# A state-space scan and a gated feed-forward on one core: one weight piece joined by halves, a clip moved to VectorE, state decays moved to ScalarE

## Chip, core and metric

The kernel runs on one core of a Trainium2 chip. The metric is the device time of one execution in microseconds, as the median of several runs; lower is better. The profile shows one further execution. Its own time is the span from the first to the last instruction plus what lies around it.

## What is computed

The first half is a chunked state-space scan over x, a, B and C (4 batches, 8 heads, 768 positions, head size 32, state size 16); the second is a feed-forward with a sigmoid gate on its 3072 x 256 result. Cut to what matters:

```python
log_a = np.log(np.clip(a, 1e-06, 1.0))
for c in range(nc):                                  # chunks of 32 positions
    cum = np.cumsum(la, axis=-1)
    L = np.exp(cum[:, :, :, None] - cum[:, :, None, :]) * causal
    M = np.einsum('bhin,bhjn->bhij', Cc, Bc) * L
    y_intra = np.einsum('bhij,bhjd->bhid', M, xc)
    y_inter = np.einsum('bhin,bhnd->bhid', Cc, state) * np.exp(cum)[:, :, :, None]
    y[:, :, sl] = y_intra + y_inter
    state = decay_full * state + np.sum(Bx, axis=2)  # Bx: B x x, decayed to the chunk's end
x = y.transpose(0, 2, 1, 3).reshape(B * S, H * D)    # 3072 x 256
h = x @ w_in                                         # 256 x 2048
g = h * (1.0 / (1.0 + np.exp(-1.702 * h)))
return (g @ w_out).astype(np.float32)                # 2048 x 256
```

The two weight matrices and their product are the bulk of the arithmetic. The weights arrive as 64-bit floats.

## The kernel before

The positions are taken in six blocks of 512 rows (`g` from 0 to 5): 128 positions of each of the four batches. Within a block the scan works in two sides of 64 positions (`i` 0 and 1) and in pairs of batches (`p`; `PG` = 2 pairs make a block). For each block there is a scan part and a feed-forward part, and the scan of block g+1 is laid between the feed-forward matmuls of block g. All engines keep the order in which the program was written: `in_order` at the end ties each instruction to the one before it on its engine.

**The weights.** VectorE has to make 32-bit floats out of the 64-bit words. The columns come in ten pieces (`PIECES`): four of two column tiles and two of four for `w_in` (column tiles f = 0 to 15), four of four for `w_out`. Pieces 0 to 3 hold f = 0 to 7, piece 4 holds f = 8 to 11, piece 5 holds f = 12 to 15. For one piece the steps are `fields` step 0 (L203, the exponent's bits), `fields` step 1 (L206, the mantissa's bits), `clamp` on ScalarE (two instructions, L224 and L226), `rounded` (L231) and `join` (L245 puts the sign in, L251 writes the finished weights). `narrow(i)` runs `rounded` on piece i, `fields` step 0 of the next piece, `join` of piece i, and `fields` step 1 of the next. For pieces 2 and 4 the join is cut into two halves of two column tiles, but the rounding ahead of them covers the whole piece. When a join is done, the next piece is fetched into the buffer that has come free (`NEXT`, on SP's queue).

**The first block.** Its feed-forward is a plain one. `hidden(0, f)` (L809) makes column tile f of the hidden layer, two accumulation steps of two matmul passes each (for the late f cut into two or four column parts), and ScalarE applies the gate (L813). It takes one of the four PSUM banks named `ff`, so tile f waits for the gate of tile f-4. After certain f the dictionary `in_hidden[0]` holds work to be issued: after f = 4 the second half of the first states, the loads of block 1's C and B by POOL's queue and `narrow(4)`; after f = 5 `store_a`; after f = 6 `pick_a(PG)` and `narrow(5)`; after f = 9 `fan_all(PG)` (matmuls L411 and scans L449), `narrow(6)` and SP's loads of block 1's x and spread a. After the sixteen tiles, `project_all(0)` (L907) goes over f again, with the work of `in_project[0]` in between.

**The clipped decay factors.** `az1` (128 x 128) and `az` (32 x 768, all of a) are read by two loads on SP and clipped by POOL in one loop, L376 and a memset of each half-chunk's first column, L378. `pick_a` reads `az1`. `store_a` writes `az` to a scratch in HBM, on SP's queue; `spread` later reads the scratch back on SP's queue, broadcast over partitions, and the scans `decay` (L403) run over it. `az1` serves the first pair of block 1, so that it need not wait for the scratch.

**The states.** `decayed(g, i)` multiplies the state before side i by the decay over that side (L671, into the only buffer of the tile `old`). `carry_first` adds it to side 1 of block 0's state (L994, through `plus`); `keep(g, i)` combines it with the block's own increment (L688, two instructions), and `keep_both` does both sides. `weigh(p)` multiplies the decay matrix of a pair by the scores that TensorE made into the PSUM area `cb` (L629). `finish` then forms y: `inter` (L730) from the states, `intra` (L746) from the weighted decay matrices. For block 1 and later y lies in the same PSUM area as the scores (`area`, one buffer), so `inter` of block 1 can't start before both `weigh` calls have read the scores.

**The start.** `finish` for block 0 runs early, with `dense` fillers on TensorE (L432: two passes over 256 columns that write into unused halves of the y banks). `spare` is one of them: it stands between the copy of the first side (L758) and `inter`.

Of the kernel before, what the change touches and what calls it, by code (L numbers as in the profile page):

```python
# [16 lines left out]
P = 128  # L17
# [18 lines left out]
def kernel(  # L36
# [31 lines left out]
    nc = tc.nc  # L68
# [159 lines left out]
    def rounded(i, half=None):  # L228

        cols = columns(i, half)  # L230
        nc.vector.scalar_tensor_tensor(out=mantissa[i][:, cols].bitcast(FP32), in0=bits[i][0][:, cols],  # L231
                                       scalar=2.0 ** -32, in1=mantissa[i][:, cols],
                                       op0=ALU.mult, op1=ALU.add)
# [4 lines left out]
    def join(i, parts=1, only=None):  # L238

        name, f, n = PIECES[i]  # L240
        n //= parts
        low, m, p2 = bits[i][1], mantissa[i], power[i]
        for k in range(parts) if only is None else only:
            cols, fs = slice(k * n * DM, (k + 1) * n * DM), slice(f + k * n, f + (k + 1) * n)
            nc.vector.scalar_tensor_tensor(out=p2[:, cols], in0=low[:, cols], scalar=0x80000000,  # L245
                                           in1=p2[:, cols], op0=ALU.bitwise_and, op1=ALU.bitwise_or)
            if name == "in":
                dst, h = w_in[:, fs].rearrange("p f k e -> p (f k e)").unsqueeze(1), 1
            else:
                dst, h = w_out[:, :, fs].rearrange("p c f e -> p c (f e)"), 2  # L250
            nc.vector.scalar_tensor_tensor(  # L251
                out=dst, in0=m[:, cols].bitcast(FP32).rearrange("p (h e) -> p h e", h=h),
                scalar=2.0 ** -20, in1=p2[:, cols].bitcast(FP32).rearrange("p (h e) -> p h e", h=h),
                op0=ALU.mult, op1=ALU.mult)
        if k == parts - 1:
            for n in NEXT.get(i, ()):
                fetch(n)

    def narrow(i):
        rounded(i)  # L260
        if i > 2 and i + 1 < len(PIECES):
            fields(i + 1, (0,))
        join(i, 2 if i in (2, 4) else 1)
        if i + 1 < len(PIECES):
            fields(i + 1, (1,) if i > 2 else range(2))

# [104 lines left out]

    fans, flat = {}, {}

    def clip(t):

        nc.gpsimd.tensor_scalar(out=t, in0=t, scalar1=1e-6, scalar2=1.0,  # L376
                                op0=ALU.max, op1=ALU.min)
        nc.gpsimd.memset(t.rearrange(by_chunk, s=2)[:, :, :, 0], 0.0)  # L378

    def pick_a(p):  # L380

# [285 lines left out]
    def decayed(g, i):  # L667

        t = ssd.tile([P, NB, Q * D], FP32, tag="old", name=f"old{g}_{i}", bufs=1)
        e = i * H + H - 1  # L670
        nc.vector.tensor_tensor(out=t, in0=state[g][:, 0] if i else state[g - 1][:, 1],  # L671
                                in1=since[g][:, :, e:e + 1].to_broadcast([P, NB, Q * D]),
                                op=ALU.mult)
        return t
# [21 lines left out]
    def finish(pairs, steps=range(2)):  # L696


        g, first = divmod(pairs[0], PG)
        early = pairs[0] < PG  # L700
        if 0 in steps:
            if early:
                banks = begun_y["banks"] = [bank(f"y0_{i}") for i in range(4)]
                y = [t[:, :2 * P].rearrange("p (k i) -> p k i", i=H) for t in banks]
                begun_y[0] = [[y[2 * t + i] for t in range(NK)] for i in range(2)], set()
            else:
                both = area(f"y{pairs[0]}")[:, :, :len(pairs) * 2 * H].rearrange(
                    "p (s t) (k i) -> p s t k i", s=2, i=H)
                begun_y[pairs[0]] = [[both[:, i, t] for t in range(NK)] for i in range(2)] + [both], set()
        y, begun = begun_y[pairs[0]]  # L710

        def begin(i, t, parts):
            new = not begun & {(i, t, q) for q in parts}
            begun.update((i, t, q) for q in parts)
            return new

        def inter(n, p, ts=range(2)):

            b = place(p)[1]
            for k in range(2):  # L720
                for i in range(2):
                    if g == 0 and i == 0:
                        continue
                    old = (state[g][:, 0] if i else state[g - 1][:, 1])[:, b + k]
                    for r in range(R):
                        t = r // 2
                        if t not in ts:
                            continue
                        rows, to = slice(32 * r, 32 * r + 32), Q * D * (r % 2)
                        nc.tensor.matmul(  # L730
                            out=y[i][t][to:to + Q * D, 2 * n + k], lhsT=old[rows],
                            rhs=st[p]["CsT"][rows, k, SIDES[i]],
                            start=begin(i, t, range(Q * (r % 2), Q * (r % 2) + Q)), stop=early,
                            tile_position=(32 * r, to), skip_group_check=True)

        def spare():
            dense(begun_y["banks"][1][:, 2 * P:], 4, False)

        def intra(n, p, ts=range(2)):
            L = Ls[p]  # L740
            for k, t in [(k, t) for t in ts for k in range(2)] if early else [
                    (k, t) for k in range(2) for t in ts]:
                for q in range(HB):
                    h = t * HB + q
                    for i, side in enumerate(SIDES):
                        nc.tensor.matmul(  # L746
                            out=y[i][t][D * q:D * q + D, 2 * n + k], lhsT=rx[p][side, k, h],
                            rhs=L[side, k, h // Q, h % Q],
                            start=begin(i, t, (q,)), stop=not early, tile_position=(H * i, D * q),
                            skip_group_check=True)  # L750

        cols = slice(2 * first * P, 2 * (first + len(pairs)) * P)

        if first == 0 and g not in yT:
            yT[g] = ffn.tile([P, NK, TG], FP32, tag="yT", name=f"yT{g}")
        if early:
            def copied(i, t):
                nc.scalar.activation(  # L758
                    yT[g][:, t, cols].rearrange("p (k s i) -> p s k i", s=2, i=H)[:, i], y[i][t],
                    AF.Copy)  # L760

            if 0 in steps:
                for t in range(NK):
                    dense(begun_y["banks"][0][:, 2 * P:])
                    intra(0, pairs[0], (t,))
                return
            for t in range(NK):
                intra(1, pairs[1], (t,))
                copied(0, t)
                if t == 0:  # L770
                    spare()
                for n, p in enumerate(pairs):
                    inter(n, p, (t,))
                copied(1, t)
        else:
            for step in steps:
                for n, p in enumerate(pairs):
                    (inter, intra)[step](n, p)
            if 1 not in steps:
                return  # L780
            for i in range(2):
                nc.scalar.activation(  # L782
                    yT[g][:, :, cols].rearrange("p t (k s i) -> p s t k i", s=2, i=H)[:, i], y[2][:, i],
                    AF.Copy)
        state.pop(g - 1, None)
        for p in pairs:
            st.pop(p)
            Ls.pop(p)
# [336 lines left out]
    rows = a.rearrange("b h s -> (b h) s")  # L1125
    nc.sync.dma_start(out=az1[:, 0], in_=rows[:, P:2 * P].unsqueeze(0).to_broadcast([R, NB * NH, P]))
    nc.sync.dma_start(out=az.rearrange("p c s -> p (c s)"), in_=rows)
    for t in az1, az:
        clip(t)
    fields(0, (1,), 0)  # L1130
    rounded(0, 0)
    finish(range(PG), (0,))
# [30 lines left out]
            nc.sync.dma_start(out=scratch[:, i].rearrange("c r i -> r c i"), in_=az[:, :, side])  # L1163

    at(in_hidden[0], 4, lambda: gain(range(PG), (1,)), lambda: keep_first(1))
    at(in_hidden[0], 5, store_a)
    at(in_hidden[0], 4, lambda: load_blocks(1, "C", [nc.gpsimd], held=True),
       lambda: load_blocks(1, "B", [nc.gpsimd]))
    at(in_hidden[0], 6, lambda: pick_a(PG))
    at(in_hidden[0], 9, lambda: fan_all(PG))  # L1170
    for i, k, c in ((2, 1, 1), (3, 2, 2), (4, 4, 4), (5, 6, 8), (6, 9, 12), (7, 12, 15)):
        at(in_hidden[0], k, lambda i=i: narrow(i))
        at(in_hidden[0], c, lambda i=i: clamp(i + 1))
    at(in_hidden[0], 9, lambda: load(PG, "x"), lambda: load(PG + 1, "x"), lambda: spread(PG + 1),
       lambda: spread_rows(1), lambda: spread_rows(2))
# [6 lines left out]
       lambda: ends_turned(PG + 1), lambda: mask_blocks(PG), lambda: mask_blocks(PG + 1),  # L1182
       lambda: clip_rows(1), lambda: decay_rows(1), lambda: since_start(PG, nc.gpsimd),
       lambda: since_start(PG + 1, nc.gpsimd), lambda: narrow(9))
    at(in_project[0], 9, lambda: score(pairs), lambda: gain(pairs), carry_first, lambda: keep_both(1),
       lambda: weigh(PG), lambda: weigh(PG + 1))
    at(in_project[0], 13, lambda: finish(pairs, (0,)))
    at(in_project[0], 15, lambda: finish(pairs, (1,)))
    at(in_project[0], 13, lambda: mix_in(1),
# [198 lines left out]
```

## Time and profile before

| | |
|---|---|
| runs shown | 350.62, 349.68, 349.15 us; median 349.68 |
| profiled execution | 349.98 us, of which the span is 348.3 us |
| TensorE (PE) | 343.3 us busy, 99% of the span; granted clock 1.000 |
| weight loads (PEld) | 281.9 us, 81%, beside the matmuls |
| VectorE (DVE) | 257.7 us, 74% |
| ScalarE (ACT) | 150.1 us, 43% |
| POOL | 46.0 us, 13% |
| HBM | 21.99 MB read, 3.24 MB written |

The share of PE is a modelled one: the matmuls are pipelined, and their ends are set by a model. A stretch in which PE is reported as busy can still hold a short stop, and a stop is best read from the starts of successive matmuls. The averages of the other engines hide that VectorE is nearly full from the start to some 90 us and half idle at the end.

### The profile page before, as it was taken

To read this page: it belongs to the slowest core of one execution; us is meant where nothing else is said; L and a number is where in the kernel's file an instruction comes from. 1 tells how busy PE (TensorE), PEld (TensorE's weight loads), DVE (VectorE), ACT (ScalarE), POOL (GpSimd) and SP (SyncE) were. 2 spreads that over 40 slices of the span, in tenths; PEclk is the share of its full clock that TensorE was granted. 3 is DMA by queue.
4 is the path that set the end of the run, shared out by engine and by line. 5 is a ranking of instruction groups with operands and counts; after the bars stand their busy time and mean duration, and the time that the engine had idled before them with its cause. 6 is when DMAs were issued, how large, how long until landed. Compare 5 with 4: busy or idle time off the path is not lost.

```text
span 348.3 us, 8552 instructions
## 1 busy us (share of the span) xinstructions
PE 343.3 (99%) x3514; PEld 281.9 (81%) x3514; DVE 257.7 (74%) x486; ACT 150.1 (43%) x335; POOL 46.0 (13%) x82
## 2 busy tenths in 40 slices
PE   9999999999999999999999999999999999999996
PEld 6658974555788888888888888888888888899996
DVE  7899999999799897839985648985554654455463
ACT  6579664005354314744342543432444322554320
POOL 8305910300396000000000000000000000000000
PEclk9999999999999999999999999999999999999999
DMA  4699985614639000554122345120000120000221
GB/s 102 197 321 279 284 167 123 98 48 79 100 77 145 2 0 13 88 115 94 27 37 61 47 98 102 23 31 9 2 4 0 19 32 12 0 2 0 33 31 60
DMA packets 82831, 25.79 MB, mean 74 GB/s; under 512 B 68856, under 2 KB 81144, under 8 KB 82792
## 3 DMA queue, kind: packets, MB, share of 16 engines
q1 hardware_dynamic: 79912, 23.19, 31.3%
q0 software_dynamic: 1888, 1.74, 2.4%
q8 instruction: 27, 0.44, 0.5%
q10 hardware_dynamic: 992, 0.33, 0.4%
q14 instruction: 12, 0.10, 0.1%
HBM read 21.99 MB, written 3.24 MB: 72 GB/s over the span
## 4 chain that ended last, share of the span: by engine, by line
PE 92%; DVE 4%; DMA 1%; issue 1%; ACT 0%; POOL 0%; SPq 0%; DVEq 0%
PE acc L967 28%; PE X L865 19%; PE Y L875 14%; PE o L907 8%; PE acc L974 7%; PE h L809 6%; PE y L746 2%; PE cb L618 2%; PE y L730 2%; DMA bits<-in_moe_w_in_dram 1%; PE A L649 1%; DVE w_in L251 1%; DVE p L245 1%; DVE p L203 1%; PE ab L520 1%
## 5 line engine op out<-in xcount | busy, mean ns | idle before, releaser
L870 ACT ACTIVATE ac<-X 128x256 f32<-128x256 f32 x76 | 29.2, 384 | 79.7 <-PE X L865 79.3
L967 PE MATMUL acc<-mg,mw 128*128 128x256 f32 x192 | 54.5, 379 | 0.0
L994 DVE TENSOR_TENSOR gT<-Y,ac 128x512 f32<-128x512 f32 x38 | 26.2, 690 | 36.9 <-PE Y L875 33.5
L842 ACT ACTIVATE gT<-gT 128x512 f32<-128x512 f32 (+1 forms) x76 | 39.4, 520 | 31.7 <-DVE gT L994 31.0
L865 PE MATMUL X<-my,mi 128*128 128x256 f32 x152 | 45.1, 379 | 0.0
L994 DVE TENSOR_TENSOR gT<-Y,b 128x256 f32<-128x256 f32 x38 | 15.9, 419 | 34.1 <-PE Y L875 34.1
L967 PEld LDWEIGHTS acc<-mg,mw 128*128 128x128 f32 x192 | 36.5, 190 | 5.0
L809 PE MATMUL h<-yT,w_in 128*128 128x128 f32 (+2 forms) x202 | 36.8, 340 | 0.6 <-DVE w_in L251 0.6
L967 PE MATMUL acc<-gT,w_out 128*128 128x256 f32 x128 | 35.5, 379 | 0.0
L809 PEld LDWEIGHTS h<-yT,w_in 128*128 128x128 f32 x202 | 27.6, 191 | 8.7 <-issue 5.9
L865 PEld LDWEIGHTS X<-my,mi 128*128 128x128 f32 x152 | 28.0, 190 | 3.8
L907 PE MATMUL o<-gT,w_out 128*128 128x512 f32 x64 | 28.6, 597 | 0.0
L833 DVE TENSOR_TENSOR mg<-gT 128x512 f32<-128x512 f32 x40 | 27.3, 682 | 0.0
L967 PEld LDWEIGHTS acc<-gT,w_out 128*128 128x128 f32 x128 | 24.2, 190 | 3.4 <-ACT yT L782 0.2
L870 ACT ACTIVATE b<-X 128x256 f32<-128x256 f32 x38 | 14.6, 385 | 20.6 <-PE X L865 20.2
L865 PE MATMUL X<-yT,w_in 128*128 128x256 f32 x76 | 23.2, 389 | 0.0
L875 PE MATMUL Y<-yT,w_in 128*128 128x256 f32 x76 | 22.7, 381 | 0.0
L875 PE MATMUL Y<-my,mi 128*128 128x256 f32 x76 | 22.6, 379 | 0.0
L865 PE MATMUL X<-my,w_in 128*128 128x256 f32 x76 | 22.6, 381 | 0.0
L875 PE MATMUL Y<-yT,mi 128*128 128x256 f32 x76 | 22.5, 379 | 0.0
L907 PEld LDWEIGHTS o<-gT,w_out 128*128 128x128 f32 x64 | 11.8, 190 | 13.2 <-issue 12.4
L1026 POOL DMA_DIRECT2D out_dram<-ob x32 | 17.4, 553 | 26.4 <-DVE ob L1021 26.1
(146 smaller groups left out, 582.5 us busy)
## 6 DMA issues: line engine op xcount, KB each, us to landing
a<-scratch SPq DMA_DIRECT2D x18, 256.0 KB
bits<-in_moe_w_out_dram SPq DMA_DIRECT2D x8, 512.0 KB
x<-in_x_dram SPq DMA_DIRECT2D x20, 128.0 KB
bits<-in_moe_w_in_dram SPq DMA_DIRECT2D x8, 256.0 KB
bits<-in_moe_w_in_dram SPq DMA_DIRECT2D x4, 512.0 KB
out_dram<-ob SPq DMA_DIRECT2D x128, 16.0 KB
af<-in_a_dram SPq DMA_DIRECT2D x20, 64.0 KB
zC<-in_C_dram SPq DMA_DIRECT2D x36, 32.0 KB
```

Of the source, the lines that this page charges most:

```text
L618: nc.tensor.matmul(out=s["cb"][side, r, k].rearrange("p (q i) -> p q i", q=Q), lhsT=BT[rows, k, side], rhs=CT[rows, k, :, side], start=Tru ...
L809: nc.tensor.matmul(out=h[:, cols], lhsT=w_in[:, f, k], rhs=yT[g][:, k, cols], start=(k == 0 and e == 0), stop=(k == NK - 1), skip_group_ch ...
L833: nc.vector.tensor_tensor(out=t[:, 0:2], in0=B[:, :, 1], in1=B[:, 0], op=ALU.subtract)
L842: nc.scalar.activation(o, i, AF.Silu, scale=GELU_SCALE)
L865: nc.tensor.matmul(out=s["X"], lhsT=lhsT, rhs=rhs, start=i == "1", stop=i == "4", skip_group_check=True)
L870: nc.scalar.activation(copy, s["X"], AF.Copy)
L875: nc.tensor.matmul(out=o, lhsT=lhsT, rhs=rhs, start=s.pop("new", False), stop=i != "5", skip_group_check=True)
L907: nc.tensor.matmul(out=o[c], lhsT=w_out[:, c, f], rhs=gT[g, f // 2][:, f % 2], start=(f == 0), stop=(f == NF - 1), skip_group_check=True)
L967: nc.tensor.matmul(out=acc[g][0][i], lhsT=w, rhs=h, start=(j == 0 and (i, 0) in begins), stop=(j == NF // 2 - 1), skip_group_check=True)
L974: nc.tensor.matmul(out=o[k] if type(o) is list else o[:, cols], lhsT=h[:, cols], rhs=w, start=(j == 0 and (i, k) in begins), stop=(j == NF ...
L994: nc.vector.tensor_tensor(out=o, in0=v, in1=w, op=ALU.add)
L1026: (nc.sync if g else nc.gpsimd).dma_start(out=rows[:, b, :, cols], in_=t[32 * r:32 * r + 32, b * P:(b + 1) * P].rearrange("p (u e) -> p u ...
```

## The change

`narrow(4)` is written out: the rounding of piece 4 is cut into halves as the join already was, so that the first half goes through `rounded`, (`fields` step 0 of piece 5), `join` before the second half is rounded. The clip of `az` moves from POOL to VectorE and from before the hidden layer to just after `narrow(5)`, and `store_a`, which reads it, moves behind it; `az1` stays on POOL. For blocks 0 and 1, `decayed` is four ScalarE copies with a per-partition scale, one for each batch, in place of one VectorE multiplication; this touches `carry_first` and the two sides of `keep(1, ...)`. The order behind them becomes `weigh(PG)`, `keep(1, 0)`, `weigh(PG + 1)`, `keep(1, 1)`. The filler `spare` is dropped, and a `dense` into the first y bank is issued instead inside `intra` of the second pair, between the rows of its first and second batch.

```diff
     def narrow(i):
+        if i == 4:
+            for k in range(2):
+                rounded(i, k)
+                if k == 0:
+                    fields(i + 1, (0,))
+                join(i, 2, (k,))
+            fields(i + 1, (1,))
+            return
         rounded(i)
...
-        join(i, 2 if i in (2, 4) else 1)
+        join(i, 2 if i == 2 else 1)
...
-    def clip(t):
+    def clip(t, engine=nc.gpsimd):
...
         e = i * H + H - 1
+        if g < 2:
+            for b in range(NB):
+                nc.scalar.activation(t[:, b], (state[g][:, 0] if i else state[g - 1][:, 1])[:, b],
+                                     AF.Copy, scale=since[g][:, b, e:e + 1])
+            return t
...
-        def spare():
-            dense(begun_y["banks"][1][:, 2 * P:], 4, False)
...
+                if early and n and not t and k:
+                    dense(begun_y["banks"][0][:, 2 * P:])
...
-                if t == 0:
-                    spare()
...
-    for t in az1, az:
-        clip(t)
+    clip(az1)
...
-    at(in_hidden[0], 5, store_a)
...
+        if i == 5:
+            at(in_hidden[0], k, lambda: clip(az, nc.vector), store_a)
...
-    at(in_project[0], 9, lambda: score(pairs), lambda: gain(pairs), carry_first, lambda: keep_both(1),
-       lambda: weigh(PG), lambda: weigh(PG + 1))
+    at(in_project[0], 9, lambda: score(pairs), lambda: gain(pairs), carry_first, lambda: weigh(PG),
+       lambda: keep(1, 0), lambda: weigh(PG + 1), lambda: keep(1, 1))
```

More of the change, by code (lines that the diff above doesn't have):

```diff
@@ L372 @@
     fans, flat = {}, {}
-    def clip(t):
-        nc.gpsimd.tensor_scalar(out=t, in0=t, scalar1=1e-6, scalar2=1.0,
+    def clip(t, engine=nc.gpsimd):
+        engine.tensor_scalar(out=t, in0=t, scalar1=1e-6, scalar2=1.0,
                                 op0=ALU.max, op1=ALU.min)
-        nc.gpsimd.memset(t.rearrange(by_chunk, s=2)[:, :, :, 0], 0.0)
+        engine.memset(t.rearrange(by_chunk, s=2)[:, :, :, 0], 0.0)
     def pick_a(p):
```

## The prediction

> **What bounds the kernel now.** I read the busy shares first, then who waited for whom on PE, then the two places in the timeline where PE stopped.
>
> ```profile
> PE 343.3 (99%) x3514; PEld 281.9 (81%) x3514; DVE 257.7 (74%) x486; ACT 150.1 (43%) x335; POOL 46.0 (13%) x82
> ...
> DVE  7899999999799897839985648985554654455463
> ```
>
> PE is the bound nearly everywhere, and the change takes no matmul away. It can gain only where PE stops, and VectorE, full for its first 90 us, is the likely cause there. The waits of PE over the whole span are few:
>
> ```profile
> PE busy L439 <- PEq L1372: 0.8, 1, 0.8
> PE h L809 <- DVE w_in L251: 0.6, 1, 0.6
> ```
>
> The second line is the one that the change aims at. In the timeline from 28 to 34 us (start, length, engine, line):
>
> ```profile
> 28.61 1.22 DVE L231 SCALAR_TENSOR_TENSOR m<-bits,m 128x1024 f32<-128x1024 uint32 x1
> ...
> 29.75 0.78 DVE L203 TENSOR_SCALAR p<-bits 128x1024 uint32<-128x1024 uint32 x1
> ...
> 30.45 0.68 DVE L245 SCALAR_TENSOR_TENSOR p<-bits,p 128x512 uint32<-128x512 uint32 x1
> ...
> 30.91 2.84 POOL L376 TENSOR_SCALAR az<-az 32x768 f32<-32x768 f32 x1
> 31.16 1.20 DVE L251 SCALAR_TENSOR_TENSOR w_in<-m,p 128x512 f32<-128x512 f32 x1
> ...
> 32.51 1.69 PE L809 MATMUL h<-yT,w_in 128*128 128x128 f32 x13 [0.56 <-DVE w_in L251]
> ```
>
> Tile f = 8 starts when L251 has written the first half of piece 4 (31.16 + 1.20 = 32.36). PE's last matmuls before it started at 31.33, 31.44, 31.55 and 31.67, so the next was due at 31.78; it came 0.73 us late, and its successor took another 0.07 to fall back into step. **The stop costs 0.80 us.** Two things make it: 1024 columns are rounded where 512 were needed, and L251 took 1.20 instead of the 0.69 that its twin at 33.00 took; it started 0.25 us after POOL's long clip.
>
> The second stop is too short for the list of waits. The timeline before 73 us:
>
> ```profile
> 65.59 7.13 PE L907 MATMUL o<-gT,w_out 128*128 128x512 f32 x16
> ...
> 70.32 2.34 DVE L629 TENSOR_TENSOR L<-L,cb 128x1024 f32<-128x1024 f32 x2
> ...
> 72.81 1.35 PE L730 MATMUL y<-CsT,S 32*64 32x64 f32 x64
> ```
>
> Sixteen matmuls 0.43 apart from 65.59, with 0.1 for the switch at each end, make L730 due at 72.66. It came at 72.81: its PSUM area is the one that both `weigh` read, and these ended at 70.32 + 2.34 = 72.66. **This stop costs 0.15 us now**, and it would swallow anything that PE gains earlier unless VectorE comes earlier too.
>
> **Piece 4 by halves, and the clip off POOL: -0.80.** Times below are from start to start, since VectorE's instructions overlap a little. Rounding 512 columns takes 0.60 (25.35 to 25.95) against 1.14 for 1024 (28.61 to 29.75); L203 0.61 alone (25.95 to 26.56), 0.70 beside POOL's clip of `az1`; L245 0.72 and L251 0.61 (26.56, 27.28, 27.89). So from 28.61: rounding to 29.21, `fields` of piece 5 to 29.91 (taken at 0.70, since `az1` is still clipped by POOL), L245 to 30.63, L251 ends at 30.63 + 0.69 = 31.32. PE wants f = 8 at 31.78, less about 0.1 for the semaphore and the weight load: 0.35 us to spare. (VectorE's wait for the words of piece 5 ended at 29.06 in the trace, so they are there by 29.21, with 0.15 in hand; later words would eat into the 0.35.) Either half of the edit alone would leave little of the stop: the split alone ends L251 at 31.3 to 31.85, the clip alone at 31.85.
>
> What is late next? f = 9 needs the bank of f = 5, whose gate ScalarE ends at 33.39; f = 9 is then due at 31.78 + 1.82 = 33.60. That holds, narrowly, since ScalarE's own chain (clamp from 30.57 to 32.9) isn't moved. f = 10 needs the second half: L231, L245, L251 end near 32.65, PE comes there at 35.4. f = 12 needs piece 5: VectorE is 0.54 ahead by the rounding of piece 5 (33.80 against 34.34), so its join ends at 38.0; PE comes at 39.7 instead of 40.5.
>
> The clip of 32x768 on VectorE lies behind `narrow(5)`: between L489 (512 columns, 0.42) and L203 (1024, 0.69), say 0.57, and 0.07 for the memset (L493), 0.65 with their gaps. Queued behind it are the scans L449, `narrow(6)` and all of VectorE's list to 72 us. It spends the 0.54 just won: VectorE stands 0.1 later than before from 39 us on. `narrow(6)` ended at 45.62 for an f that PE takes at 47.68, 46.9 now: covered by over 1 us.
>
> On SP's queue `store_a` (0.82 us of issue at 34.38) moves behind the fetch at 37.33, to about 39.2, and x, the spread `a` and the rows `af` stand behind it:
>
> ```profile
> 38.32 7.33 SPq L146 DMA_DIRECT2D x<-in_x_dram  x4
> 45.75 2.02 SPq L282 DMA_DIRECT2D a<-scratch  x2
> 47.81 5.19 SPq L292 DMA_DIRECT2D af<-in_a_dram  x8
> ```
>
> They go 1 to 2 us later. The first readers on VectorE are the scan of `a` at 57.98 and L489 at 60.70, 10 us behind their issue; cost nothing. On POOL's queue the sixteen loads of C and B, which started at 34.62 behind the clip, start near 31.
>
> **The decays on ScalarE: they keep the 0.80 and add 0.15.** Off VectorE go three L671 (67.17, 68.08, 69.27; 0.45 to 0.54 from start to start): 1.4. Each becomes four copies of 128x64; no row has that shape. Bounds: 0.20 (128x1, L314) and 0.29 from start to start (128x128, L388), so 0.8 to 1.2 a decay, taken at 1.1, near the wider row, since a copy's fixed part weighs most. ScalarE has nothing from 58.6 to 79.2, so the first one is long done. From 67.28 on VectorE: `plus` to 67.74, `weigh` (1.13) to 68.87, L688 (68.62 to 69.27, 0.65) to 69.52, `weigh` to 70.65, ending about 70.75 instead of 72.66. The new waits are of L688: its decay starts when `plus` has ended (67.7) and takes to 68.8, so the first `weigh` hides it; the second is hidden by the second `weigh` to within 0.2. Behind a waiting L688 stand the `weigh` and so L730. PE wants the area at 72.66 - 0.80 = 71.86, less 0.1. Margin: 0.8 to 1.0. Both stops are then gone. Without this part 70.32 + 2.34 + 0.1 would hold PE to its old time, and the 0.80 would be lost.
>
> **The filler: 0.** PE's two passes at 14.50 to 15.13 (0.63) leave their place ahead of `inter` and come where PE waits for the second `weigh` of the pair: the rows before end near 13.61, the rows behind start at 13.90. They would then start near 14.35, 0.45 later, and `inter` 0.15 to 0.2 earlier. PE reaches `hidden` that much earlier, but f = 1 follows L251 at 17.89 (0.42), and that follows a DMA:
>
> ```profile
> 17.22 0.29 DVE L203 TENSOR_SCALAR p<-bits 128x256 uint32<-128x256 uint32 x1 [0.52 <-DMA bits<-in_moe_w_in_dram]
> ```
>
> f = 1 starts at 18.56 on time, when weights ready at 18.31 allow 18.45 at best; and f = 3 follows its own join (21.98) at 22.13. Bounds: 0.1 won, 0.2 lost if the rows come later than that; I take 0.
>
> **Sum:** -0.80 - 0.15 + 0 = -0.95. The profiled execution goes from 349.98 (span 348.3) to 349.03 (span 347.35). It lies 0.30 above the median of the runs, 349.68, so the forecast is 348.7. A measurement can tell about 0.5% (1.75 us) from no change: the gain, 0.27%, is under that.
>
> **Rivals.** *The wait moves to the score area* (349.6): if L688 waits for ScalarE, `weigh` ends later than 71.75 and L730 takes back what f = 8 gave. To lose all, a decay must take about 2 us, 0.5 a copy; no row of ScalarE up to 128x128 shows over 0.40. 0.12.
>
> *POOL's remaining clip blocks VectorE* (349.9, slower). The clip of `az1` starts at 29.24 and lasts 1.44, and `fields` of piece 5 now starts just there. If VectorE had to stand still for all of it, L203 would start at 30.7, L251 would end at 32.76, f = 8 would come at 32.87, 0.36 later than now; with the 0.15 won at 72, +0.2. It decides from 0.35 us of blocking on. Against it: L203 beside that clip took only 0.09 more than alone, and within the long clip the L245 at 32.28 and the L251 at 33.00 took 0.68 and 0.69; the most seen is the 0.51 of one L251. 0.10. The Trainium skill, SBUF — State Buffer, section Who interferes with whom, says that the two engines share a port pair and that the later one "fully blocks" until the earlier is done. By that rule this rival would be the forecast; but also the L251 at 31.16 should have stood until 33.75, and it ended at 32.36, so the trace agrees only in that there is interference.
>
> *The start gains too* (348.1): the filler's whole 0.63 comes off the path, if the first weights come earlier by chance of the DMA. 0.06.
>
> *The weights' DMA is pushed back* (350.6 and more): POOL's sixteen loads, 0.5 MB, now come 3.6 us earlier into a stretch where the DMA share is 0.92 to 1.04 and 290 to 305 GB/s move. The join of piece 5 stands behind `fields` of piece 6 on VectorE (due 34.9); if that piece lands after 36.6, f = 12 is late by as much, and beyond 37.6 the gain is gone. All sixteen loads ahead of it would cost 0.5 MB / 290 GB/s = 1.8 us, and L203 at 35.48 didn't wait. 0.08, half of it within 0.5%.
>
> **The numbers.** Forecast 0.64. The range 348.0 to 350.0 holds the forecast, the first three rivals and the partial losses between; it leaves out the last one and a gain over 1.7. Over 0.5% faster (below 347.9) is the far half of the start's rival (0.03) and a little for what the trace can't show: 0.04. Over 0.5% slower is the far half of the last rival (0.04) and as little: 0.05. Between: 0.91.
>
> **What would show it.** Right: no wait of PE on L251 near 32 us, f = 8 at 31.8; L251 of f = 8 at 0.69; VectorE's last `weigh` before 71.2 and L730 at 71.9; everything behind 0.95 earlier. Wrong: f = 8 still waits; L688 idles on ScalarE by more than 0.5; `hidden` starts after 16.8; a granted clock below 1.00 near 14 to 20 us.

## The result, and the profile after

| | before | after |
|---|---|---|
| time, median (us) | 349.71 (349.06 to 351.27, 17 runs) | 348.40 (347.87 to 349.6, 17 runs) |
| profiled execution, time / span (us) | 349.98 / 348.3 | 347.87 / 346.1 |

The ratio is 0.9963, with an interval of 0.9949 to 0.9977: 1.3 us less (0.8 to 1.8). That is under the 0.5% that the prediction took as the least to be told from no change, but the interval leaves no change out. The forecast was 348.7. Ratios here and below compare executions in the chip's usual state; the one of `early_piece1` that was profiled (2000 us) was not in it, so its trace is not read.

The first line of the page and the whole list of PE's waits in the kernel after:

```profile
PE 341.6 (99%) x3514; PEld 281.4 (81%) x3514; DVE 256.3 (74%) x486; ACT 152.5 (44%) x347; POOL 42.1 (12%) x80
...
PE busy L447 <- PEq L1382: 0.9, 1, 0.9
PE ab L528 <- DVE cum L377: 0.4, 1, 0.4
```

As many matmuls as before. The wait on L251 is gone from the list; a small one on L377, in a later stage, is new here, but a second trace of the same kernel doesn't have it. The timeline near f = 8:

```profile
27.63 0.69 DVE L231 SCALAR_TENSOR_TENSOR m<-bits,m 128x512 f32<-128x512 uint32 x1
28.04 1.12 POOL L384 TENSOR_SCALAR az<-az 128x128 f32<-128x128 f32 x1 [14.90 <-DMA az<-in_a_dram]
28.24 0.78 DVE L203 TENSOR_SCALAR p<-bits 128x1024 uint32<-128x1024 uint32 x1
28.95 0.68 DVE L245 SCALAR_TENSOR_TENSOR p<-bits,p 128x512 uint32<-128x512 uint32 x1
29.66 0.69 DVE L251 SCALAR_TENSOR_TENSOR w_in<-m,p 128x512 f32<-128x512 f32 x1
...
27.32 7.22 PE L819 MATMUL h<-yT,w_in 128*128 128x256 f32 x52
```

One half is rounded, the field of piece 5 is cut beside POOL's clip of `az1`, and L251 takes 0.69 and ends at 30.35. PE's hidden matmuls (last line) run through from 27.32 to 34.54 without a gap, f = 8 among them. The clip that VectorE has taken over, and SP's queue:

```profile
37.66 0.56 DVE L384 TENSOR_SCALAR az<-az 32x768 f32<-32x768 f32 x1
38.27 0.67 DVE L457 TENSOR_TENSOR_SCAN L<-ab,idents 128x256 f32<-128x256 f32 x1
...
38.38 0.82 SPq L1172 DMA_DIRECT2D scratch<-az  x2
39.24 5.33 SPq L146 DMA_DIRECT2D x<-in_x_dram  x4
44.68 1.49 SPq L290 DMA_DIRECT2D a<-scratch  x2
```

The clip holds VectorE's list for 0.61 us. The issue of `store_a` moved 4 us, but the spread `a`, which reads what it stored, is issued no later than before (44.68 against 45.75; counted from A, the mark explained below, 0.1 earlier), where the prediction had 1 to 2 us later. The score area of block 1, which PE takes over at `inter`:

```profile
63.82 7.13 PE L917 MATMUL o<-gT,w_out 128*128 128x512 f32 x16
...
66.68 1.21 DVE L637 TENSOR_TENSOR L<-L,cb 128x1024 f32<-128x1024 f32 x1
66.79 1.06 ACT L681 ACTIVATE old<-S,since 128x64 f32<-128x64 f32 x4 [8.01 <-DVE S L1004]
67.89 0.61 DVE L701 SCALAR_TENSOR_TENSOR S<-A,part,old 128x128 f32<-128x128 f32 x2
68.41 1.21 DVE L637 TENSOR_TENSOR L<-L,cb 128x1024 f32<-128x1024 f32 x1
68.59 1.06 ACT L681 ACTIVATE old<-S,since 128x64 f32<-128x64 f32 x4 [0.74 <-DVE S L701]
...
70.88 1.16 PE L743 MATMUL y<-CsT,S 32*64 32x64 f32 x64
```

Each decay takes ScalarE 1.06 us beside a `weigh` of 1.21, and no L701 waits. The second `weigh` ends at 69.62. Before, PE came 0.15 us after the `weigh` that held it (72.66 to 72.81), so it could have ended at 70.73 and not held PE: 1.11 us in hand.

**Where the time went.** The start differs from one execution to the next, so whole spans are poor evidence. I take one mark behind it: A, the first of the state matmuls that follow f = 4 (line L649 before, L657 after). Over all traces A lies between 24.9 and 26.8 us. The table counts from there: A to the first `inter` matmul of block 1, from that to the first matmul behind those 64, and all the rest (us, from the matmuls' records):

| kernel | A at | A to `inter` | the 64 | the rest |
|---|---|---|---|---|
| before | 25.88 | 46.92 | 1.28 | 274.19 |
| after | 24.91 | 45.97 | 1.09 | 274.16 |
| after, second trace | 25.33 | 45.97 | 1.09 | 274.17 |

The two traces of the changed kernel agree to 0.01, and the rest is what it was to within 0.03. Of the kernel before there is one trace. A to `inter` lost 0.95, and the 64 matmuls, which follow a stop before and none after, lost 0.19: **1.14 us in all**, against 1.3 (0.8 to 1.8) by the medians. Of the 2.1 us between the two profiled executions, the other 1.0 lies ahead of A.

### The profile page after: what moved, and what is told of

The parts are those of the page before. It is cut to its first block, busy times and chain, and to the rows that moved or that the text cites. A ratio compares the mean times of both kernels' runs of the same rounds, so it can differ in the third digit from the quotient of the medians.

```text
span 346.1 us, 8565 instructions
## 1 busy us (share of the span) xinstructions
PE 341.6 (99%) x3514; PEld 281.4 (81%) x3514; DVE 256.3 (74%) x486; ACT 152.5 (44%) x347; POOL 42.1 (12%) x80
## 4 chain that ended last, share of the span: by engine, by line
PE 97%; ACT 1%; ACTq 1%; DVE 0%; issue 0%
PE acc L977 28%; PE X L875 19%; PE Y L885 14%; PE h L819 10%; PE o L917 8%; PE acc L984 7%; PE y L758 3%; PE cb L626 2%; PE y L743 2%; PE A L657 1%; PE ab L528 1%; ACTq L130 1%; PE y L440 0%; ACT L322 0%; PE b L584 0%; ACT cum L373 0%
## 5 line engine op out<-in xcount | busy, mean ns | idle before, releaser
L411 DVE TENSOR_TENSOR_SCAN L<-a,idents 128x1024 f32<-128x1024 f32 x9 | 20.5, 2274 | 0.0
```

What stands on the lines that cost most here:

```text
L411: nc.vector.tensor_tensor_scan(out=L, data0=ra[p].rearrange("p k e -> p (k e)"), data1=idents.rearrange("p h i -> p (h i)"), initial=0.0, ...
```

## The experiments

My theory was that two stops hold PE, at f = 8 and at `inter`, and that the first is worth nothing while the second stands, because VectorE's `weigh` gives it back. The rivals were that the gain is the filler's, at the start, and that POOL's remaining clip takes some of it. I added each part to the kernel before, took each away from the kernel after, and then parted order and engine of the decays. All ratios are against the kernel before, run beside each group, so its median differs a little from group to group. Two sets are small: `order_only` has 7 runs and `no_filler` 5, the others 11 or more.

**Piece 4 by halves alone** (`split_only`): the kernel before with the new branch in `narrow`.

```diff
     def narrow(i):
+        if i == 4:
+            for k in range(2):
+                rounded(i, k)
+                if k == 0:
+                    fields(i + 1, (0,))
+                join(i, 2, (k,))
+            fields(i + 1, (1,))
+            return
```

> The kernel before, with only piece 4 rounded and joined by halves. Theory 1 (the gain of the change is two stops of PE, 0.80 us before tile f = 8 and 0.34 us at inter of block 1, and the filler gives nothing): the first half of piece 4 is joined 0.5 to 1.1 us earlier, so the stop before f = 8 falls from 0.80 to 0.1 or less; VectorE is 0.5 us ahead from there on (no clip is added to it), so the stop at inter doesn't swallow the gain but grows from 0.15 to about 0.35 us; in all 0.4 to 0.6 us faster than before. Theory 2 (half or more of the gain comes from the start, where the filler was moved): 0.3 us or less. If POOL's long clip slows whichever join instruction it meets by 0.5 us, L245 or L251 of the first half still takes 1.2 us.

Measured: 350.24 against 350.04, ratio 1.0004 (0.9985 to 1.0023). A miss. PE's wait at f = 8 is gone, but a longer one stands at `inter`; from its waits and its timeline:

```profile
PE y L738 <- DVE L L637: 1.7, 1, 1.7
...
31.50 3.20 POOL L384 TENSOR_SCALAR az<-az 32x768 f32<-32x768 f32 x1
32.00 1.31 DVE L245 SCALAR_TENSOR_TENSOR p<-bits,p 128x512 uint32<-128x512 uint32 x1
33.34 0.69 DVE L251 SCALAR_TENSOR_TENSOR w_in<-m,p 128x512 f32<-128x512 f32 x1
33.95 1.30 DVE L206 TENSOR_SCALAR m<-bits 128x1024 uint32<-128x1024 uint32 x1
```

POOL's long clip now met two other instructions: L245 took 1.31 instead of 0.69 and L206 1.30 instead of 0.69, while the L251 between them kept its 0.69. That is 1.2 us of VectorE's time, and it had also waited longer for words (0.77 us at 26.17; the stop of PE at f = 6 that followed cost 0.75, so PE came to f = 8 late by that much). The trace doesn't part these two; either way the delay was carried on for 40 us to the `weigh`.

**The clip alone** (`clip_only`): `clip(az)` and `store_a` as in the change, the rest as before.

> The kernel before, with only the clip of az on VectorE behind the join of piece 5 and the scratch store behind it. Theory 1: L251 of the first half of piece 4 takes 0.69 instead of 1.20 us, f = 8 comes 0.5 us earlier with a stop of 0.2 to 0.3 left; but VectorE pays 0.65 us for the clip, stands 0.1 us later than before at the scores, and PE waits there 0.6 to 0.8 us; in all no change, -0.1 to +0.2 us. Theory 2: no change either. If the loads behind the store on SP's queue come too late, VectorE idles before the scan at 58 us, and it is slower by that idle time.

Measured: 349.71 against 350.04, ratio 0.9992 (0.998 to 1.0003), as expected. L251 took 0.69 and the stop at f = 8 shrank from 0.80 to 0.32 (A to the fan-out matmuls, L411, took 9.88 against 9.56 without a stop). PE then stopped further on:

```profile
72.66 1.29 PE L730 MATMUL y<-CsT,S 32*64 32x64 f32 x64 [0.84 <-DVE L L629]
```

**The filler alone** (`filler_only`): only `spare` goes and `dense` comes into `intra`.

> The kernel before, with only the filler moved from ahead of inter into the second rows. Theory 1: hidden starts 0.1 to 0.5 us earlier, measured from the first score matmul, but f = 1 to f = 3 then wait for their weights, and the stop before f = 8 takes up whatever is left; no change, -0.1 to +0.1 us. Theory 2: 0.4 to 0.7 us faster.

Measured: 350.02 against 350.04, ratio 0.9994 (0.9981 to 1.0007), as expected. From the first score matmul to the first hidden matmul PE took 7.10 us instead of 7.58. Here that ended in a wait for the next words, which landed late:

```profile
18.14 0.29 DVE L203 TENSOR_SCALAR p<-bits 128x256 uint32<-128x256 uint32 x1 [1.49 <-DMA bits<-in_moe_w_in_dram]
```

**Without the new decays and order** (`no_decay`): the kernel after with `keep_both(1)` ahead of both `weigh` and the decays on VectorE.

> The changed kernel, with the decays of the states back on VectorE and the old order behind them (both sides of the state, then both weigh). Theory 1: f = 8 without a stop, 0.80 us won; VectorE ends the second weigh at its old time or 0.1 us later, so PE stops about 0.95 us before inter of block 1 and all but 0.1 us of the gain is given back; in all -0.2 to +0.1 us against the kernel before. Theory 2: 0.6 us or more remain, since the start was won before that.

Measured: 350.12 against 350.04, ratio 0.9998 (0.9987 to 1.0008), as expected. There is no stop at f = 8 (A to the fan-out matmuls takes 9.56); all of it comes back here:

```profile
72.31 1.16 PE L738 MATMUL y<-CsT,S 32*64 32x64 f32 x64 [1.04 <-DVE L L637]
```

So without the third part nothing is kept of the gain, but this part has two halves, the engine and the order.

**The order alone** (`order_only`): the kernel after without the branch that sends the decays to ScalarE. **The new decays and order alone** (`decay_only`): both halves put into the kernel before. **ScalarE in the old order** (`act_old_order`): the kernel after with this line back:

```diff
-       lambda: keep(1, 0), lambda: weigh(PG + 1), lambda: keep(1, 1))
+       ..., lambda: keep_both(1), lambda: weigh(PG), lambda: weigh(PG + 1))
```

> The changed kernel with the three decays back on VectorE, but in the new order behind them (weigh, side 0, weigh, side 1). Theory 1, sharpened by the runs so far (before the change PE is held at inter of block 1 by VectorE's unbroken chain, which runs from the landing of piece 1 to the second weigh; what shortens that chain counts until PE's own work is the longer): the new order takes one of the two state sides from ahead of the second weigh, two decays of about 0.48 us come back ahead of it; VectorE frees the scores about 0.2 us before PE wants them, so this kernel is as fast as the changed one, 1.0 to 1.3 us faster than before. Rival (moving the decays off VectorE is what matters): PE stops 0.5 us or more at inter, and no more than 0.7 us is won.

> The kernel before with only the decays on ScalarE and the new order. Theory 1: VectorE's chain is 2.2 us shorter, so inter of block 1 has no stop and its matmuls start at full pace; the stop before f = 8 stays at about 0.8 us; in all 0.3 to 0.6 us faster. Rival (VectorE's chain is all that counts, and the stop before f = 8 is nothing by itself): 1.0 us or more.

> The changed kernel with the decays on ScalarE, but the old order behind them (both sides of the state, then both weigh). Theory 1 (the new order, not the engine, frees the scores in time): nothing covers the 1.1 us that four copies take on ScalarE, so VectorE waits for them twice, about 2 us in all; the second weigh ends 1.5 us after PE wants the scores, PE stops there by that, and this kernel is 0.3 to 0.8 us slower than the one before. Rival (taking the decays off VectorE is what matters): 0.7 us or more faster than before.

Measured, `order_only`: 348.39 against 349.62, ratio 0.9967 (0.9955 to 0.998), as fast as the whole change, as expected. Its timeline:

```profile
70.10 0.61 DVE L696 SCALAR_TENSOR_TENSOR S<-A,part,old 128x128 f32<-128x128 f32 x2
70.63 1.21 DVE L637 TENSOR_TENSOR L<-L,cb 128x1024 f32<-128x1024 f32 x1
...
71.76 0.42 DVE L679 TENSOR_TENSOR old<-S,since 128x256 f32<-128x256 f32 x1
...
72.23 1.16 PE L738 MATMUL y<-CsT,S 32*64 32x64 f32 x64
```

The second decay (L679 at 71.76) stands behind the `weigh` instead of ahead of it. The `weigh` ends at 71.84, 0.24 us before it would hold PE; PE doesn't wait.

Measured, `decay_only`: 349.36 against 349.62, ratio 0.9994 (0.9982 to 1.0007); 0.3 less, where 0.3 to 0.6 was expected; the medians can't tell so little. The trace can. Behind the start this is PE's only wait:

```profile
PE h L814 <- DVE w_in L251: 0.6, 1, 0.6
```

There is no stop at `inter`, the one at f = 8 is as before, and from A to the end it takes 0.37 less.

Measured, `act_old_order`: 351.57 against 350.13, ratio 1.0038 (1.002 to 1.0056), 1.3 us slower than before. That is more than the 0.3 to 0.8 expected. From A to the end its trace is 0.68 longer; what it lost ahead of A (26.84, with 1.64 of waiting for words) can't be told from the scatter of the start. The timeline shows where the 0.68 comes from:

```profile
69.81 0.61 DVE L701 SCALAR_TENSOR_TENSOR S<-A,part,old 128x128 f32<-128x128 f32 x2 [1.13 <-ACT old L681]
71.61 0.61 DVE L701 SCALAR_TENSOR_TENSOR S<-A,part,old 128x128 f32<-128x128 f32 x2 [1.19 <-ACT old L681]
72.13 2.34 DVE L637 TENSOR_TENSOR L<-L,cb 128x1024 f32<-128x1024 f32 x2
```

With nothing between a decay and its reader, VectorE stands still for each, 2.3 us, and both `weigh` queue behind that. The decays on ScalarE are an advantage only in an order that hides them, and there they aren't needed.

**The filler in its old place, and none at all** (`no_filler_move`, `no_filler`): the kernel after with `spare` back, and without `dense` in `intra`.

> The changed kernel with the filler back in its old place ahead of inter. Theory 1: hidden starts 0.2 to 0.5 us later, counted from the first score matmul; up to f = 3 the weights hold PE as long, so the time is that of the changed kernel within 0.2 us, 1.0 to 1.3 us faster than before. Rival (with no later stop left to swallow it, an early hidden counts in full): 0.4 to 0.6 us slower than the changed kernel, 0.7 us faster than before.

> The changed kernel without the moved filler at all (that one dense is left out; it computes nothing that is used). Theory 1: hidden starts 0.3 to 0.5 us earlier still, and f = 1 to f = 3 wait for their weights; the time is that of the changed kernel within 0.2 us. Rival of the run before: 0.4 us faster than the changed kernel. If the filler keeps the clock up, the granted clock falls below 1.00 in the first 25 us and it is over 1 us slower.

Measured: 348.56 and 348.48, both against 349.62; ratios 0.9975 (0.9962 to 0.9988) and 0.9966 (0.9954 to 0.9978). Both intervals hold the change's own ratio. PE came to `hidden` 0.73 later than in the changed kernel and 0.12 earlier, counted from the first score matmul; neither lies where it was expected, and the time didn't follow. The granted clock of the run without the filler is 1.00. The filler isn't where the gain is.

**Weights asked for earlier** (`early_fetch`, `early_piece1`): the kernel after with the second half of piece 0 and piece 1 released ahead of the first `weigh`, and with only piece 1 released earlier, right behind piece 0. These try to win what the start loses to late words.

```diff
+    fetch(0, held=nc.vector, halves=(1,))
+    fetch(1, held=nc.vector)
...
-    fetch(0, held=nc.vector, halves=(1,))
...
-    fetch(1, held=nc.vector)
```

> The changed kernel with the loads of the second half of piece 0 and of piece 1 released ahead of the first weigh instead of behind it. Theory 1: with both later stops gone, what is left to vary is the start, and there VectorE waits for the words of piece 1 (0 to 1.5 us in the traces so far); the words come about 1.3 us earlier, the wait goes, tile f = 4 ends at 24.9 to 25.1 us in the trace, and the median is 0.3 to 0.7 us under the changed kernel's. Against it: the loads of x share the DMA engines then, and the first intra may wait for them; then no gain or a loss up to 0.5 us.

> The changed kernel with the load of piece 1 released right behind that of piece 0's second half, ahead of the two products of the end rows. Theory 1: piece 1 lands about 0.6 us earlier; half of the gain of the run before, 0.1 to 0.4 us under the changed kernel, without touching the loads of x.

Measured: 348.81 and 348.92 against 350.13; ratios 0.9967 (0.9951 to 0.9984) and 0.9968 (0.9955 to 0.9981). Both miss: they are no better than the change itself, whose ratio beside them (`after_again`) was 0.9964 (0.9949 to 0.9979). In `early_fetch` the wait for piece 1 is gone, but VectorE waited 0.40 us for words at 25.82 instead, which cost PE 0.3 between A and `inter`.

> The changed kernel once more, on the same chip as the three others, to compare them with it. Theory 1: from the state matmuls after f = 4 to the end the trace takes 321.2 us, as in the first trace of it; the time up to there is between 24.8 and 26.3 us.

All kernels by the same marks (us):

| kernel | A at | A to `inter` | the 64 | the rest |
|---|---|---|---|---|
| `split_only` | 25.25 | 48.50 | 1.14 | 274.16 |
| `clip_only` | 25.47 | 47.20 | 1.22 | 274.18 |
| `filler_only` | 26.80 | 47.11 | 1.12 | 274.19 |
| `no_decay` | 25.23 | 47.08 | 1.09 | 274.20 |
| `act_old_order` | 26.84 | 47.79 | 1.09 | 274.19 |
| `decay_only` | 25.61 | 46.77 | 1.09 | 274.16 |
| `early_fetch` | 25.36 | 46.28 | 1.09 | 274.16 |
| `order_only` | 26.26 | 45.97 | 1.09 | 274.20 |
| `no_filler_move` | 25.45 | 45.97 | 1.09 | 274.18 |
| `no_filler` | 25.55 | 45.97 | 1.09 | 274.16 |

The trace of `after_again` is the second one in the first table; from A it took 321.2 us, as expected. 45.97 is what PE needs with no stop. `decay_only` has 0.80 more, exactly the stop at f = 8; before has 0.95 more, both stops. The kernels without the new order have 0.95 to 2.5 more, whatever else they do: there VectorE's list, not PE's, sets when `inter` starts.

## Why the prediction was right, and where it was not

- **The stop at f = 8, -0.80: right.** From A to the fan-out matmuls (L411, L419) PE took 10.36 before and 9.56 after. Its sub-terms held: L251 0.69, `fields` of piece 5 in 0.71 (taken at 0.70), the clip on VectorE 0.61 (0.65).
- **What would keep it: the mechanism right, the credit wrong.** "Without this part 70.32 + 2.34 + 0.1 would hold PE to its old time, and the 0.80 would be lost": `no_decay` shows that. But the part was credited to ScalarE: it was costed as "Off VectorE go three L671", 1.4 us of decays sent to ScalarE. What it needed was the other half: the decay and sum of the second side, moved behind the second `weigh`. Before, they took VectorE 1.05 us, from 69.27 to 70.32, ahead of both:

```profile
69.27 0.42 DVE L671 TENSOR_TENSOR old<-S,since 128x256 f32<-128x256 f32 x1
69.79 0.61 DVE L688 SCALAR_TENSOR_TENSOR S<-A,part,old 128x128 f32<-128x128 f32 x2
```

`order_only` has that alone and gains as much; `act_old_order` has ScalarE alone and loses. What ScalarE adds is time in hand, 1.11 instead of 0.24, which nothing here uses. The terms were close: a decay 1.06 (taken at 1.1), the time in hand 1.11 (0.8 to 1.0).

- **The stop at `inter`, -0.15: mis-sized.** It was worth 0.34 in the one trace of the kernel before. The 0.15 is there (0.95 less 0.80), but the 64 matmuls behind the stop also took 1.28 instead of 1.09, 0.19 that the sum left out. For f = 8 the 0.07 of falling back into step had been counted; here nobody looked at the matmuls behind the stop. The sum would have been -1.14, a median of 348.5.
- **The halves and the clip, singly.** "Either half of the edit alone would leave little of the stop" held for the clip, with 0.32 left; in `split_only` PE came to f = 8 too late to tell. The sentence said nothing on what VectorE brings to `inter`, which is what decided: neither was faster. Whether one of the two would do, with the new order behind it, was not run.
- **The filler, 0: right to what the medians can tell, with wrong steps.** From the first score matmul to `hidden` PE took 7.1 to 7.5 us in the seven traces with the filler in its new place and 7.3 to 7.8 in the five with it in its old one, on the mean 0.37 less, not 0.15 to 0.2. What comes of that depends on the words: from the first score matmul to A it took 16.2 to 16.5 us in four of the seven (one of them `early_fetch`, which asks for its words earlier) and 17.5 to 18.0 in three, and 16.5 to 16.7 in the five. Whether the new place has anything to do with the late words in those three traces, or chance alone, stays open.
- **The rivals.** VectorE waited for ScalarE's decays, and PE at the score area because of it, only in `act_old_order`, where nothing stands between a decay and its reader. POOL's remaining clip did not stop VectorE: `fields` inside it took 0.78 against 0.69 alone, and the rival needed 0.35. The Trainium skill, SBUF — State Buffer, section Who interferes with whom, would have the later engine wait for the whole of the other's instruction where the two share a port, and counts VectorE instructions with two inputs from SBUF among those that contend; these traces don't show such a wait: within the one POOL clip of 3.20 us in `split_only` an L251 with two inputs took its usual 0.69, and the L245 that was held took 0.62 longer, though the clip had 2.70 us to run when it began. The weights' DMA pushed back by POOL's loads didn't show: PE has no stop from A to `inter` in the kernel after, and f = 12 lies between.
- **The range.** 348.0 to 350.0 holds the old median (349.71) too, so that the new one lies in it says little. What bears the forecast out is that both stops are gone and the runs that part them.
- **What stays open.** The traces explain 1.14 of a measured 1.3, whose interval reaches from 0.8 to 1.8. The start could hold the difference; its scatter of 1.9 us over the traces is too large to say.

## What to carry to other kernels

Follow the engine that made the bound engine wait to the next place where the two meet: what is won at the first stop comes back at the second unless that engine's list gets shorter up to there too. Before sending work to another engine, look whether it need stand ahead of the release at all: moving it behind cost nothing here and gained as much, and the other engine helped only with something to hide its latency. Where the start of a kernel scatters by more than the effect, measure from a mark behind it and count the time up to the next free-running mark.

## What the runs showed of the hardware

- **Work on POOL lengthens some VectorE instructions and not others.** Four traces have the 32x768 clip on POOL (2.84 to 3.20 us). Inside it L251 took 1.20 (in two traces), L203 1.31 and L245 1.31, against 0.69 each; these were the first to start inside the clip, each in its trace. Of the later ones a single L206 was held (1.30 against 0.69). So each that is held costs about 0.5 to 0.6 us, the first ones far less than the 2.6 to 2.7 us that the clip had left; why, no run shows.
- **The same happens in every trace just ahead of `inter`.** Beside POOL's two multiplications L604 (L612 in the kernel after) L245 and L251 take 1.75 and 1.63; the same shapes take 1.22 at 36.09 and 37.34. In the kernel before:

```profile
62.89 3.28 POOL L604 TENSOR_TENSOR CsT<-Ct,since 128x256 f32<-128x256 f32 x2 [15.85 <-DVE since L499]
63.84 1.75 DVE L245 SCALAR_TENSOR_TENSOR p<-bits,p 128x1024 uint32<-128x1024 uint32 x1
65.62 1.63 DVE L251 SCALAR_TENSOR_TENSOR w_out<-m,p 128x1024 f32<-128x1024 f32 x1
```

That is 0.94 us on the very list of VectorE that held PE at `inter`. No run moved this work.

- **After a stop small matmuls were not always at full pace, at a granted clock of 1.00.** The 64 `inter` matmuls took 1.28 after a stop of 0.15 us and 1.09 after none; but 1.22 after 0.84, and again 1.09 after 1.04. So the stop's length doesn't set it. More than half of the 0.19 stands in one place: the twelfth matmul started 0.12 behind the eleventh, 0.07 in the run with 1.22, and 0.01 in the others. What does it is open.
- **Thirteen readable traces, with little changed in the first 16 us, differ by 1.9 us at A.** What differs most is when the next words land: VectorE waited 0 to 1.6 us for those of piece 1.
